# Linear attention gated by a squared-ReLU MLP: masks later on GpSimd, and three small matmul groups in another tile mode

## The chip, the cores and the metric

The kernel runs on one core of a Trainium2 chip. The metric is the time of one execution on the device, in microseconds (us): the median of several runs. Durations of single instructions come from one profiled execution, in which times count from the start of the span (first to last instruction of the core). The engines are named as the profile names them: PE is TensorE (PEld its weight loads), DVE is VectorE, ACT is ScalarE, POOL is GpSimd, and SP is the queue that issues nearly all DMAs.

## What is computed

For 2048 tokens of width 448, in bfloat16 (weights wqkv, wo, w1, w2; 16 heads of 28; hidden width 1792):

```python
xn = _layernorm(x, axis=-1)
q, k, v = heads(xn @ wqkv)
phi = lambda t: jnp.where(t > 0, t + 1, jnp.exp(t)) + 1e-6
kv = jnp.einsum("bhsd,bhse->bhde", phi(k), v)
z = jnp.einsum("bhsd->bhd", phi(k))
num = jnp.einsum("bhqd,bhde->bhqe", phi(q), kv)
den = jnp.einsum("bhqd,bhd->bhq", phi(q), z)[..., None] + 1e-6
s = merge_heads(num / den) @ wo
r = relu(xn @ w1 + b1)
g = silu((r * r) @ w2 + b2)
return x + s * g
```

(`heads` and `merge_heads` stand for the reshapes of the reference.)

## The kernel before

**Tiling.** The tokens are 16 tiles of 128 (index si), in 4 groups of 512 (g) or 2 halves of 1024 (u). The width 448 is three blocks of 128 and a rest of 64 (c = 0 to 3). The normalized tile xn has 512 columns: its last 64 are stored twice, so that after transposition the rest lies on rows 0 to 63 of block 3 of xT and again on rows 64 to 127. The weights' rest rows are loaded twice too (`load_k`, lines 420 to 426), once into each half. Two 64-row matmuls on two different results can so run side by side on the two halves of TensorE; `pe_four` (line 509) does that for four results at a time.

**Stages.** Line 1108 runs 43 matmuls on a zero tile (`wz`) ahead of the real work. Tiles 0 to 3 are normalized on VectorE (`ln_stats` 465, `ln_norm` 483, the copy of the 64 columns in `dup` 713) and transposed on TensorE (`x_transpose0` 726, matmuls of line 737, copies back in lines 757 and 763); later tiles are transposed by DMA (line 500). The first hidden units H0.0 to H0.6 are computed in pieces (`pe_part` 572, matmuls of line 701), as soon as parts of xT and of w1 are there. Then follow, in groups of four results, K (phi(k), token-major, line 622), Q (phi(q), transposed, line 646) and H (hidden units, line 705), with the first four gates G (line 977) among them. ScalarE takes the exponentials and the ReLU, VectorE the rest of phi (lines 605 and 612), the squares (686) and the gate's sum with b2 (994).

**q rests.** Column block 384 to 447 of q, the fourth of the transposed q, has only 64 output rows. `qx(u)` (line 653) computes it for even tiles into PSUM rows 0 to 63 and for odd tiles into rows 64 to 127, side by side. Its contraction runs over three 128-row blocks, and over rows 0 to 63 of the fourth.

**z.** GpSimd adds up phi(k) over the 16 tiles (`zsum`, line 628; sums of line 632, the last into `zb`). `z_cols` (line 840) turns zb into columns by matmuls against a column of ones: three with 128 columns of zb (line 846) and two with the 64 of the rest, for rows 0 to 63 and 64 to 127 (line 851). Three VectorE products (line 863) with `zmask` spread them over heads into `zsb`, the weights of `den` (line 895, matmuls of line 900).

**Masks.** `zmask`, `hmask` (used in `fold_wv`, line 832) and `ehd` (used in `spread`, line 938) are made of memsets on VectorE and 14 `affine_select` on GpSimd (line 359): eight for zmask, four for ehd, two for hmask. They are added to the program right after the identity and have no wait for any other work but their memsets.

**The last gate.** For tile 15 the bias b2 is added on TensorE: `gg` with `part` (line 967) begins with one matmul of a row of ones (`onesr`) and row 0 of `b2b` (line 975), then the 14 matmuls of the gate, in two pieces between the last output matmuls (line 1067). SiLU reads the result from PSUM (line 989).

**Order.** The program is a list of operations with reads and writes. The order on PE and SP is the order of the list. For ACT, DVE and POOL a list scheduler (`schedule`, line 88) with an estimated cost for each operation picks the order, the eight PSUM banks, and the engine where there is a choice. An engine carries out its list strictly in order, and an operation waits for the semaphores of what it needs.

Of the kernel before, what the change touches and what calls it, by code (L numbers as in the profile page):

```python
# [6 lines left out]
ALU = mybir.AluOpType  # L7
AF = mybir.ActivationFunctionType

P = 128  # L10
S, D, F = 2048, 448, 1792
NT, NG, NF = S // 128, S // 512, F // 128
NH, DH = 16, 28
# [281 lines left out]
def bass_recurrent_scan__linear_attn_block__dense_activation_squared_relu__prompt_kernel(  # L295
    nc, A_x, A_wqkv, A_wo, B_x, B_w1, B_b1, B_w2, B_b2, out
):
    with ExitStack() as es:
# [8 lines left out]
        zmask = sb("zmask", [P, 5, 32], f32)  # L307
        ones = sb("ones", [P, 1], bf)
        wz = sb("wz", [P, P], bf)
        onesr = sb("onesr", [1, P], bf)  # L310
        ehd = sb("ehd", [P, D], bf)
        x_tok = sb("x_tok", [P, NT, D], bf)
        xn = sb("xn", [P, NT, 512], bf)
        xT = sb("xT", [P, NT, 4, P], bf)
        w_qkv = sb("w_qkv", [P, 4, 3 * D], bf)
# [12 lines left out]
        pqx = sb("pqx", [P, 2, 4, P], bf)  # L328
        pk = sb("pk", [P, NT, D], bf)
        zacc = sb("zacc", [P, D], f32)  # L330
        zb = sb("zb", [P, D], bf)
        at = sb("at", [P, 4, D], bf)
        eps5 = sb("eps5", [P, 1], f32)
        r2 = sb("r2", [P, NF, S], bf)
# [11 lines left out]
        def pool(fn, writes, reads=(), dur=0.3):  # L346
            add("pool", fn, reads, writes, dur)
# [4 lines left out]
        def bcast(ap, reps):  # L352
            return free_ap(ap, [[0, reps]] + list(ap.ap[1:]))

        def select(view, name, pattern, base, cm, fill, op=ALU.is_ge, dur=0.3):
            masks.append(
                add(
                    "pool",
                    lambda e, _: e.affine_select(
                        out=view, in_=view, pattern=pattern, compare_op=op, fill=fill, base=base, channel_multiplier=cm  # L360
                    ),
                    [name], [name], dur,
                )
            )

        masks = []
        pool(lambda e, _: e.memset(ident[:, :], 0.0), ["ident"])
        select(ident[:, :], "ident", [[-1, P]], 0, 1, 1.0, ALU.not_equal)
        pool(lambda e, _: e.memset(eps5[:, :], 1e-5), ["eps5"], dur=0.1)
# [1 line left out]
        def vset(ap, val, name, again=False, dur=0.08):  # L371
            add("dve", lambda e, _: e.memset(ap, val), [name] if again else [], [name], dur)

        vset(wz[:, :], 0.0, "wz")
        vset(onesr[:, :], 1.0, "onesr")
        vset(zsb[:, :, :], 0.0, "zsb0")
        vset(hmask[:, :], 1.0, "hmask", dur=0.15)
        vset(zmask[:, :, :], 1.0, "zmask", dur=0.2)
        vset(ehd[:, :], 0.0, "ehd", dur=0.3)
        vset(kvm[:, :, :], 0.0, "kvm", dur=1.0)  # L380
        pool(lambda e, _: e.memset(eps6[:, :], 1e-6), ["eps6"], dur=0.1)

        def late_constants():
            hv = hmask[:, :].rearrange("p (b j) -> p b j", b=HC)
            select(hv, "hmask", [[-DH, HC], [0, DH]], 0, 1, 0.0)
            select(hv, "hmask", [[DH, HC], [0, DH]], DH - 1, -1, 0.0)
            for view, pat, base in (
                (zmask[:, 0:3, :], [[P, 3], [-DH, 32]], 0),
                (zmask[:, 3, :], [[-DH, 32]], 384),
                (zmask[:, 4, :], [[-DH, 32]], 320),  # L390
            ):
                select(view, "zmask", pat, base, 1, 0.0)
                select(view, "zmask", [[-a, n] for a, n in pat], DH - 1 - base, -1, 0.0)
            select(zmask[:, 3, :], "zmask", [[0, 32]], 63, -1, 0.0)
            select(zmask[:, 4, :], "zmask", [[0, 32]], -64, 1, 0.0)
            pool(lambda e, _: e.memset(ones[:, :], 1.0), ["ones"], dur=0.1)
            ev = ehd[:, :].rearrange("p (h j) -> p h j", h=NH)
            for g in range(NG):
                select(ev, "ehd", [[-1, NH], [0, DH]], -32 * g, 1, 1.0, ALU.not_equal, dur=0.6)

        tok = lambda t, lo, hi: t[0].rearrange("(p s) d -> p s d", s=NT)[:, lo:hi, :]

# [56 lines left out]
            load_k("sp", w_qkv, A_wqkv, "wv", 2 * D, 3 * D)  # L459

        add("act", lambda e, _: e.preload_act_table_set("natural_log_exp_and_others"), [], ["actw"], 1.3).prio = -2000.0
        masks.clear()
        late_constants()

        def ln_stats(si, hold=()):
            op = add("dve", lambda e, _: e.bn_stats(st6[:, si, :], x_tok[:, si, :]), [("x", si)], [("st", si)], 0.58)  # L466
# [161 lines left out]
        def zsum(i):  # L628
            o = zb if i == NT - 1 else zacc
            add(  # L630
                "pool",
                lambda e, _: e.tensor_tensor(  # L632
                    out=o[:, :], in0=pk[:, 0, :] if i == 1 else zacc[:, :], in1=pk[:, i, :], op=ALU.add
                ),
                [("pk", i), ("pk", 0) if i == 1 else "zacc"], ["zb" if i == NT - 1 else "zacc"], 1.05,
            )

        for si in range(4):
            pr.alias(("xT", si), [("xTp", si // 2 * 2, c) for c in range(4)])
# [13 lines left out]
        def qx(u):  # L653
            b = Buf("QX")

            def f(e, _):
                last = None
                for c in range(4):
                    rw = slice(0, 128) if c < 3 else slice(0, 64)
                    for o in (0, 1):  # L660
                        last = e.matmul(  # L661
                            ps(b)[64 * o : 64 * o + 64, 0:512], w_qkv[rw, c, 384:448],
                            xT[rw, 8 * u + o : 8 * u + 8 : 2, c, :], start=(c == 0), stop=(c == 3),
                        )
                return last

            add("pe", f, xnames(2 * u) + xnames(2 * u + 1) + wnames("wq"), [b], 4 * MM(512) + 0.1)
            phi(b, pqx[:, u, :, :].rearrange("p a b -> p (a b)"), ("pqx", u), 512)

        def h_out(b, g, fi):  # L670
# [169 lines left out]
        def z_cols():  # L840
            b = Buf("Z")

            def f(e, _):
                last = None
                for c in range(3):
                    last = e.matmul(
                        ps(b)[:, c : c + 1], zb[:, c * P : (c + 1) * P], ones[:, :], start=(c == 0), stop=True,
                        skip_group_check=True,
                    )
                for o in (0, 1):  # L850
                    last = e.matmul(
                        ps(b)[64 * o : 64 * o + 64, 3 + o : 4 + o], zb[:, 384:448], ones[:, :], start=False, stop=True,
                        skip_group_check=True,
                    )
                return last

            add("pe", f, ["zb", "ones"], [b], 0.35)
            for v, c0, c1, lo, hi in ((0, 0, 3, 0, 128), (1, 3, 4, 0, 64), (2, 4, 5, 64, 128)):

                def zops(e, _, c0=c0, c1=c1, lo=lo, hi=hi):  # L860
                    z = ps(b)[lo:hi, c0:c1]
                    z = free_ap(z, [[1, c1 - c0], [0, 32]])
                    return e.tensor_tensor(out=zsb[lo:hi, c0:c1, :], in0=z, in1=zmask[lo:hi, c0:c1, :], op=ALU.mult)

                add("dve", zops, [b, "zmask", "zsb0"], [("zsb", v)], 0.2)


        def fold_wo(c):
            b = Buf("M")
# [25 lines left out]
        def den():  # L895
            def f(e, _):
# [16 lines left out]

            add(
                "pe", f,
                [("zsb", v) for v in range(3)] + [("pq", g, c) for g in range(NG) for c in range(3)]
                + [("pqx", u) for u in (0, 1)],
                [denb], 4 * 0.24,
            )
# [47 lines left out]
        def gg(si, b=None, part=None):  # L967
            b = b or Buf("G")
            g = si // 4
            fis = range(NF) if part is None else part  # L970

            def f(e, _):
                last = None
                if part is not None and fis[0] == 0:
                    last = e.matmul(ps(b)[:, 0:D], onesr[:, :], b2b[0:1, :], start=True, stop=False)
                for fi in fis:
                    last = e.matmul(  # L977
                        ps(b)[:, 0:D], r2[:, fi, si * P : (si + 1) * P], w_2[:, fi, :],
                        start=(fi == 0 and part is None), stop=(fi == NF - 1),
                    )  # L980
                return last

            rd = [("r2", g, fi) for fi in fis] + ["w2"] + (["b2b", "onesr"] if part is not None else [])
            add("pe", f, rd + ([b] if fis[0] else []), [b], len(fis) * MM(D) + (0.19 if part is not None else 0))
            gs = gbuf[:, si % NGB, :]
            if part is not None:
                if fis[-1] == NF - 1:
                    add(
                        "act", lambda e, _: e.activation(out=gs, in_=ps(b)[:, 0:D], func=AF.Silu), [b, "acts"],
                        [("g", si % NGB)], 0.576,  # L990
                    )
            else:
                add(
                    "dve", lambda e, _: e.tensor_tensor(out=gs, in0=ps(b)[:, 0:D], in1=b2b[:, :], op=ALU.add),  # L994
                    [b, "b2b"], [("g", si % NGB)], 0.624,
                )
# [108 lines left out]
                x_transpose(si, si + step)  # L1105
            pr.lead = 0.0

        warm(43, 0.106)
        H0 = {fi: hh(0, fi, fi >= 7) for fi in range(NF)}
        pr.hot = -100.0  # L1110
        ln_stats(0)
# [18 lines left out]
            pe_part([H0[i] for i in range(4)], 0, (c,))  # L1130
        pe_part([H0[i] for i in range(4, 6)], 0)
        t23 = x_transpose0(2)
        for op in masks:
            op.hold = [t23]
        pr.hot = None
        pe_part([H0[6]], 0)
        for c in range(3):
# [10 lines left out]
        load_w1(3, "sp", "sp")  # L1148
        load_x(8, 12)
        ln(4, 8, lead=3, hold=[t23])  # L1150
        load_x(12, 16)
        dma("sp", w_2[:, :, :], B_w2.rearrange("(f p) d -> p f d", p=P), ["w2"], F * D * 2)
        late_loads()
# [13 lines left out]
            zsum(i)  # L1167
        gg(2)
        gg(3)
        quads("H2.8 H2.9 H2.10 H2.11 Q1.1 H2.12 Q1.2 H2.13")  # L1170
        quads("K3.0 H3.0 K3.1 H3.2 K3.2 H3.1 K3.3 H3.3")
        for i in range(12, 16):
# [77 lines left out]
```

## Time and profile before

| | |
|---|---|
| median of 6 runs | 148.42 us (148.17 to 149.26) |
| the profiled execution | 148.17 us |
| its span, first to last instruction | 146.4 us |
| PE busy | 141.1 us (96% of the span) |
| DVE, ACT, POOL busy | 96.2, 79.4, 34.5 us |
| granted TensorE clock | 1.0 in the whole span |
| masks on POOL (line 359, from 1.56) | zmask 2.30, ehd 3.13, hmask 0.66 us |

The profile lists for each engine its instructions with start and duration. "Idle before <- X" names what ended the wait in front of an instruction; "issue" is a wait for nothing that the profile shows. The tile mode of a matmul or weight load stands as rows*columns ahead of its shape: 128*128 is the whole array, 128*64 a half of its columns, 64*64 a quarter. Matmuls are pipelined: starts are more telling than durations. The chain of work that ended last follows the waits back from the end.

### The profile page before, as it was taken

To read this page: it belongs to the slowest core of one execution; us is meant where nothing else is said; L and a number is where in the kernel's file an instruction comes from. 1 tells how busy PE (TensorE), PEld (TensorE's weight loads), DVE (VectorE), ACT (ScalarE), POOL (GpSimd) and SP (SyncE) were. 2 spreads that over 40 slices of the span, in tenths; PEclk is the share of its full clock that TensorE was granted. 3 is DMA by queue.
4 is the path that set the end of the run, shared out by engine and by line. 5 is a ranking of instruction groups with operands and counts; after the bars stand their busy time and mean duration, and the time that the engine had idled before them with its cause. 6 is when DMAs were issued, how large, how long until landed. Compare 5 with 4: busy or idle time off the path is not lost.

```text
span 146.4 us, 2838 instructions
## 1 busy us (share of the span) xinstructions
PE 141.1 (96%) x1127; PEld 70.2 (48%) x1127; DVE 96.2 (66%) x222; ACT 79.4 (54%) x152; POOL 34.5 (24%) x50
## 2 busy tenths in 40 slices
PE   7799999999999999999999999999999999999990
PEld 7675444444444444444443554364444545545450
DVE  6979878899978995268999310089675426136343
ACT  3618888987986980487879613997211110210200
POOL 6800026570000650001550000000001909109100
PEclk9999999999999999999999999999999999999999
DMA  3977699934802500000000000000000211102212
GB/s 85 323 229 222 150 240 377 322 107 87 61 0 43 100 4 0 0 0 4 2 0 0 4 0 0 0 7 0 0 0 0 66 64 63 63 0 63 67 63 63
DMA packets 16025, 10.53 MB, mean 72 GB/s; under 512 B 7372, under 2 KB 15628, under 8 KB 16012
## 3 DMA queue, kind: packets, MB, share of 16 engines
q1 hardware_dynamic: 15824, 10.28, 26.9%
q8 instruction: 9, 0.15, 0.5%
q10 hardware_dynamic: 188, 0.07, 0.2%
q14 instruction: 4, 0.03, 0.1%
HBM read 6.94 MB, written 1.84 MB: 60 GB/s over the span
## 4 chain that ended last, share of the span: by engine, by line
PE 93%; DVE 3%; DMA 1%; ACT 0%; issue 0%; DVEq 0%
PE pb L977 30%; PE pb L705 26%; PE pb L622 7%; PE pb L793 6%; PE pb L646 6%; PE pb L1031 6%; PE pb L701 3%; PE pb L1067 2%; PE pb L661 2%; DMA x_tok<-in_A_x_dram 1%; PE pb L799 1%; PE pb L878 1%; DVE st L466 1%; PE pb L737 1%; PE pb L938 1%; PE pb L822 1%
## 5 line engine op out<-in xcount | busy, mean ns | idle before, releaser
L977 PE MATMUL pb<-w,r 128*128 128x448 bf16 x224 | 44.3, 353 | 0.0
L672 ACT ACTIVATE r<-pb,b1f 128x512 bf16<-128x512 f32 x54 | 33.8, 690 | 10.6 <-PE pb L705 10.6
L705 PE MATMUL pb<-xT,w 64*128 64x512 bf16 (+1 forms) x291 | 38.5, 376 | 0.0
L977 PEld LDWEIGHTS pb<-w,r 128*128 128x128 bf16 x224 | 21.1, 98 | 21.1 <-issue 2.0
L1004 ACT ACTIVATE gbuf<-gbuf 128x448 bf16<-128x448 bf16 x15 | 8.5, 580 | 29.7 <-DVE gbuf L994 29.7
L632 POOL TENSOR_TENSOR zacc<-zacc,pk 128x448 f32<-128x448 f32 x13 | 14.6, 1124 | 39.8 <-DVE pk L612 36.5
L1020 POOL TENSOR_TENSOR obuf<-obuf,x_tok 128x448 bf16<-128x448 bf16 x12 | 12.0, 1031 | 48.7 <-DVE obuf L1014 48.7
L705 PEld LDWEIGHTS pb<-xT,w 64*128 64x128 bf16 (+1 forms) x291 | 14.2, 94 | 16.6 <-issue 0.4
L994 DVE TENSOR_TENSOR gbuf<-pb,b2b 128x448 bf16<-128x448 f32 x15 | 9.4, 624 | 16.6 <-PE pb L977 16.5
L686 DVE TENSOR_TENSOR r<-r 128x512 bf16<-128x512 bf16 x35 | 16.6, 513 | 3.0 <-ACT r L672 3.0
L1014 DVE TENSOR_TENSOR obuf<-pb,gbuf 128x448 bf16<-128x448 f32 (+2 forms) x17 | 9.2, 591 | 7.2 <-PE pb L1031 4.7
L622 PE MATMUL pb<-w_qkv,xT 64*128 64x448 bf16 x112 | 13.2, 349 | 0.0
L961 DVE TENSOR_TENSOR pqT<-pqT,pb 128x512 bf16<-128x512 bf16 x12 | 7.4, 682 | 8.6 <-PE pb L938 8.6
L687 ACT ACTIVATE r<-r 128x512 bf16<-128x512 bf16 x21 | 12.6, 634 | 0.0
L646 PE MATMUL pb<-xT,w_qkv 64*128 64x512 bf16 x84 | 11.0, 376 | 0.0
L705 PE MATMUL pb<-xT,w_1r 64*128 64x512 bf16 x56 | 10.3, 377 | 0.0
L612 DVE SCALAR_TENSOR_TENSOR pk<-pb,pk 128x448 bf16<-128x448 f32 x16 | 9.9, 624 | 0.5
L466 DVE BATCH_NORM_STATS2 st<-x_tok 128x6 f32<-128x448 bf16 x16 | 9.2, 615 | 1.2 <-DMA x_tok<-in_A_x_dram 1.2
L600 ACT ACTIVATE pk<-pb 128x448 bf16<-128x448 f32 x16 | 7.8, 541 | 3.9 <-PE pb L622 3.9
L793 PE MATMUL pb<-pk,xn 128*128 128x448 bf16 x48 | 9.4, 353 | 0.0
L612 DVE SCALAR_TENSOR_TENSOR pqT<-pb,pqT 128x512 bf16<-128x512 f32 x12 | 8.2, 689 | 0.3
L622 PEld LDWEIGHTS pb<-w_qkv,xT 64*128 64x128 bf16 x112 | 5.4, 94 | 6.1 <-issue 0.4
(90 smaller groups left out, 126.0 us busy)
## 6 DMA issues: line engine op xcount, KB each, us to landing
out_dram<-obuf SPq DMA_DIRECT2D x15, 112.0 KB, 1.8
w<-in_B_w_dram SPq DMA_DIRECT2D x1, 1568.0 KB, 10.1
x_tok<-in_A_x_dram SPq DMA_DIRECT2D x3, 448.0 KB, 4.1
w<-in_B_w_dram SPq DMA_DIRECT2D x3, 384.0 KB, 4.2
w_qkv<-in_A_wqkv_dram SPq DMA_DIRECT2D x3, 336.0 KB, 5.7
w_o<-in_A_wo_dram SPq DMA_DIRECT2D x1, 392.0 KB, 9.4
w_qkv<-in_A_wqkv_dram SPq DMA_DIRECT2D x6, 56.0 KB, 5.1
x_tok<-in_A_x_dram SPq DMA_DIRECT2D x2, 112.0 KB, 2.1
```

The costliest lines, as they stand in the source:

```text
L466: op = add("dve", lambda e, _: e.bn_stats(st6[:, si, :], x_tok[:, si, :]), [("x", si)], [("st", si)], 0.58)
L612: lambda e, _: e.scalar_tensor_tensor(out=slot, in0=ps(buf)[:, 0:n], scalar=1.0 + 1e-6, in1=slot, op0=ALU.add, op1=ALU.max),
L622: return e.matmul(ps(b)[:, 0:D], xT[rw, si, c, :], w_qkv[rw, c, D : 2 * D], start=start, stop=stop)
L632: lambda e, _: e.tensor_tensor(out=o[:, :], in0=pk[:, 0, :] if i == 1 else zacc[:, :], in1=pk[:, i, :], op=ALU.add),
L646: return e.matmul(ps(b)[:, 0:512], w_qkv[rw, c, m * P : (m + 1) * P], xT[rw, 4 * g : 4 * g + 4, c, :], start=start, stop=stop,)
L672: rl = lambda e, _: e.activation(out=slot, in_=ps(b)[:, 0:512], func=AF.Relu, bias=b1f[:, fi : fi + 1])
L686: return e.tensor_tensor(out=slot, in0=slot, in1=slot, op=ALU.mult)
L687: return e.activation(out=slot, in_=slot, func=AF.Square)
L705: return e.matmul(ps(b)[:, 0:512], lhs, xT[rw, 4 * g : 4 * g + 4, c, :], start=start, stop=stop, skip_group_check=not full,)
L793: last = e.matmul(ps(b)[:, 0:D], xn[:, si, c * P : (c + 1) * P], pk[:, si, :], start=(si == 0), stop=(si == NT - 1),)
L977: last = e.matmul(ps(b)[:, 0:D], r2[:, fi, si * P : (si + 1) * P], w_2[:, fi, :], start=(fi == 0 and part is None), stop=(fi == NF - 1),)
L1020: lambda e, _: e.tensor_tensor(out=ob, in0=ob, in1=x_tok[:, si, lo:hi], op=ALU.add),
```

## The change

- **Masks.** The zmask selects now wait for the last copy of the transposed tiles 2 and 3 (line 763), the ehd and hmask selects for the sum of the fourth gate (line 994, si = 3); in the built order they lie on POOL ahead of the first zacc sum, and between the sums of tile 11 and tile 12.
- **q rests.** A new tile `wqh` holds the fourth block of the q weights times 0.5, made by VectorE on both halves of the rows. The fourth pass of `qx` uses all 128 rows: both copies of the rest times half the weight each.
- **z columns.** `zb` grows to 512 columns, of which the last 64 repeat the rest (a copy on POOL). All five matmuls take 128 columns; the last two take the same ones. One VectorE product with zmask makes the whole of zsb.
- **Last gate.** The bias matmul takes the identity and all of b2b instead of one row.
- The memsets of onesr and zsb are gone, the memset of wz is put first by priority, that of ones is added earlier. The warm-up has 40 matmuls instead of 43.

On PE, SP and ACT the built order is the same but for these edits, and the PSUM banks are the same. On DVE, wqh stands after the second ReLU of line 677 and ahead of the squares.

```diff
+        wqh = sb("wqh", [P, 64], bf)
-        zb = sb("zb", [P, D], bf)
+        zb = sb("zb", [P, 512], bf)
...
         vset(wz[:, :], 0.0, "wz")
-        vset(onesr[:, :], 1.0, "onesr")
-        vset(zsb[:, :, :], 0.0, "zsb0")
+        pr.ops[-1].prio = -1e6
...
-        def late_constants():
+        def z_masks(after):
...
-                select(view, "zmask", pat, base, 1, 0.0)
-                select(view, "zmask", [[-a, n] for a, n in pat], DH - 1 - base, -1, 0.0)
+                select(view, "zmask", pat, base, 1, 0.0, after=after)
+                select(view, "zmask", [[-a, n] for a, n in pat], DH - 1 - base, -1, 0.0, after=after)
...
+        def head_masks(after):
...
-                select(ev, "ehd", [[-1, NH], [0, DH]], -32 * g, 1, 1.0, ALU.not_equal, dur=0.6)
+                select(ev, "ehd", [[-1, NH], [0, DH]], -32 * g, 1, 1.0, ALU.not_equal, dur=0.6, after=after)
...
+            if i == NT - 1:
+                pool(lambda e, _: e.tensor_copy(zb[:, D:512], zb[:, 384:D]), ["zbd"], ["zb"], dur=0.25)
...
-                    rw = slice(0, 128) if c < 3 else slice(0, 64)
                     for o in (0, 1):
                         last = e.matmul(
-                            ps(b)[64 * o : 64 * o + 64, 0:512], w_qkv[rw, c, 384:448],
-                            xT[rw, 8 * u + o : 8 * u + 8 : 2, c, :], start=(c == 0), stop=(c == 3),
+                            ps(b)[64 * o : 64 * o + 64, 0:512], w_qkv[:, c, 384:448] if c < 3 else wqh[:, :],
+                            xT[:, 8 * u + o : 8 * u + 8 : 2, c, :], start=(c == 0), stop=(c == 3),
                         )
...
+            if u == 0:
+                add(
+                    "dve",
+                    lambda e, _: e.tensor_scalar(
+                        out=wqh[:, :], in0=w_qkv[:, 3, 384:448], scalar1=0.5, scalar2=None, op0=ALU.mult
+                    ),
+                    wnames("wq"), ["wqh"], 0.1,
+                )
...
-                for c in range(3):
+                for c in range(5):
+                    k = min(c, 3) * P
                     last = e.matmul(
-                        ps(b)[:, c : c + 1], zb[:, c * P : (c + 1) * P], ones[:, :], start=(c == 0), stop=True,
-                        skip_group_check=True,
-                    )
-                for o in (0, 1):
-                    last = e.matmul(
-                        ps(b)[64 * o : 64 * o + 64, 3 + o : 4 + o], zb[:, 384:448], ones[:, :], start=False, stop=True,
+                        ps(b)[:, c : c + 1], zb[:, k : k + P], ones[:, :], start=(c == 0), stop=True,
                         skip_group_check=True,
                     )
...
+            z = lambda: free_ap(ps(b)[:, 0:5], [[1, 5], [0, 32]])
+            add(
+                "dve", lambda e, _: e.tensor_tensor(out=zsb[:, :, :], in0=z(), in1=zmask[:, :, :], op=ALU.mult),
+                [b, "zmask"], ["zsb"], 0.25,
+            )
...
-                    last = e.matmul(ps(b)[:, 0:D], onesr[:, :], b2b[0:1, :], start=True, stop=False)
+                    last = e.matmul(ps(b)[:, 0:D], ident[:, :], b2b[:, :], start=True, stop=False)
...
-        warm(43, 0.106)
+        warm(40, 0.107)
...
-        for op in masks:
-            op.hold = [t23]
...
+        z_masks([("xTp", 2, 3)])
...
+        head_masks([("g", 3)])
```

## The prediction

> **What bounds the kernel now.** I read the page's busy times first, then the chain that ended last, then TensorE's waits.
>
> ```profile
> PE 141.1 (96%) x1127; PEld 70.2 (48%) x1127; DVE 96.2 (66%) x222; ACT 79.4 (54%) x152; POOL 34.5 (24%) x50
> PE 93%; DVE 3%; DMA 1%; ACT 0%; issue 0%; DVEq 0%
> ```
>
> ```profile
> PE pb L1081 <- DVE wz L372: 1.1, 1, 1.1
> PE pb L737 <- DVE xn L486: 0.7, 1, 0.7
> ```
>
> TensorE works in 141.1 of 146.4 us and is 93% of the chain. Its only listed waits lie ahead of the first transposes (5.68). From there to 143 us it is fed without a listed gap, so the change can gain in two ways only: start that stream earlier, or take TensorE time out of it. It can lose by making TensorE wait.
>
> **Tile modes inside the stream.** A weight load shows rows*columns. The loads around the first q rest (line 661), then the matmuls around the z columns (846, 851) and around the last gate's bias (975):
>
> ```profile
> 37.34 0.36 PEld L661 LDWEIGHTS pb<-xT,w_qkv 128*64 128x64 bf16 x6 [0.42 <-issue]
> 38.11 0.11 PEld L661 LDWEIGHTS pb<-xT,w_qkv 64*64 64x64 bf16 x2 [0.41 <-issue]
> 38.45 0.11 PEld L977 LDWEIGHTS pb<-w,r 128*128 128x128 bf16 x2 [0.23 <-issue]
> ```
>
> ```profile
> 86.11 0.22 PE L846 MATMUL pb<-ones,zb 128*128 128x1 bf16 x3
> 86.25 0.19 PE L851 MATMUL pb<-ones,zb 128*64 128x1 bf16 x2
> 86.38 0.36 PE L793 MATMUL pb<-pk,xn 128*128 128x448 bf16 x1
> ```
>
> ```profile
> 138.09 0.73 PE L1067 MATMUL pb<-msb,pqT 128*128 128x448 bf16 x3
> 138.75 0.36 PE L975 MATMUL pb<-b2b,onesr 1*128 1x448 bf16 x1
> 139.04 0.36 PE L977 MATMUL pb<-w,r 128*128 128x448 bf16 x1
> ```
>
> Each change of the second number or the first is a point where the next weights are not loaded under the matmul before ("issue" idle).
>
> *q rests, twice.* A pair of 512-column matmuls streams in 0.217 (eight of line 646 take 1.03, the last alone 0.38: 0.65 over three pairs). The 64*64 pair of the rests takes 38.45 - 38.11 = 0.34, so 0.12 goes to one mode change. The change runs this pair as 128*64: three changes become two. At 78.94 the rows repeat (79.70 to 80.04: 0.34). Gain 2 x 0.12 = 0.24. A 128-row pair isn't dearer: the three ahead take 38.11 - 37.34 = 0.77 = 3 x 0.217 + 0.12.
>
> A rule speaks against this edit: the Trainium skill, "TensorEngine Tiling (Array Packing)", Theoretical Speedup, promises up to twice the speed for a contraction of 64 rows or fewer in its own tiles; its Key Properties say that a change of mode drains the engine. By the first, a 64-row pair costs half a 128-row one, 0.11, and filling it up gives 0.11 away each time: 0.24 - 0.22 leaves 0.02. The row decides: only two of the four 64*64 tiles were used, and the pair took longer than a 128-row one, not half.
>
> *z columns.* Three full-mode one-column matmuls start (0.22 - 0.163)/2 = 0.03 apart. All five take 86.38 - 86.11 = 0.27 with two mode changes; five in full mode 5 x 0.03 = 0.15. Gain 0.12 (nothing if a full weight load showed at the 0.056 spacing of the warm-up matmuls).
>
> *Last bias.* A 448-column matmul streams in 0.19 (four of line 977: 0.92, the last alone 0.35). From the third of line 1067 (138.09 + 2 x 0.19 = 138.47) to the gate's first at 139.04 are 0.57 for two of them: 0.57 - 0.38 = 0.19 gained with identity and b2b on 128 rows.
>
> These 0.55 us lie in TensorE's own stream. Everything behind, the last SiLU and line 1014 included, follows TensorE, so they should reach the end.
>
> **The start.** VectorE makes the first tiles while GpSimd writes masks:
>
> ```profile
> 4.81 0.53 DVE L722 COPY xn<-xn 128x64 bf16<-128x64 bf16 x1
> 5.24 0.38 DVE L486 TENSOR_SCALAR xn<-x_tok,mv,rstd 128x448 bf16<-128x448 bf16 x1
> ...
> 7.76 0.18 DVE L722 COPY xn<-xn 128x64 bf16<-128x64 bf16 x1
> ```
>
> The same copy of 64 columns takes 0.53 beside GpSimd's ehd selects (3.82 to 6.95) and 0.18 without them. The Trainium skill, "SBUF — State Buffer", Who interferes with whom, has it that VectorE's two-port modes and GpSimd exclude each other for a whole instruction. By that rule both line 486 too might wait, up to 0.67 each (one select); by the rows they (0.36 at 4.41, 0.38 at 5.24) are as short as later ones (0.40). I take the row: 0.35, not 1.7. The transposes at 5.68 move to 5.33.
>
> What is late next? Two transfers, whose issue and landing do not move. The first block of w1 is issued at 2.2 and lands 4.2 later, 6.4: line 701 begins at 6.45 instead of 6.66. The second:
>
> ```profile
> L404 SPq DMA_DIRECT2D w<-in_B_w_dram x1: 668/668/668, 2.8 to 2.8; - x1
> ...
> DMA to landing us min/median/max: 5.0/5.0/5.0
> ```
>
> It lands at 7.8 to 7.9. The thirteenth matmul of line 701, the first to need it, already starts at 6.66 + 12 x 0.11 = 7.98, just behind it. So 0.30 of the 0.35 turns into a wait for this block. What stays is the 0.05 that the second transposes wait for VectorE's copy (8.69, six matmuls of 0.11 after 7.98 end at 8.64). Gain 0.05; ends: 0, and 0.35 if the block lands early.
>
> **The rest, at nothing.** 43 warm-up matmuls become 40: 0.17 of filler ahead of a wait for VectorE; the remaining pause is 0.67 - 0.35 + 0.17 = 0.49, shorter than today's, after which the matmuls run at full clock. Two memsets less on VectorE end before x lands (2.70 and 2.92). The zmask selects (2.3 us) now follow the last transposed copy (10.17), beside four bn_stats, which took 0.59 to 0.63 beside selects at 2.92 to 6.46 and about as much without; zmask is needed at 86.5. The ehd and hmask selects (3.13 + 0.66) follow the fourth gate's sum (line 994, ends 58.78); queued behind them on GpSimd is the zacc sum of 68.94: 6 us to spare, without that up to 3.8. VectorE's squares at 61.37 to 63.5 may each lose up to a select (0.67); their readers come after 112, and 0.77 idle follows. The new zb copy (at most 0.3, by a small select) ends near 75.5; z columns read it at 86.1. One zsb product instead of three, with 2.4 us before line 900. SP and ACT keep their orders.
>
> **The new wait.** The halved weights (wqh) are one small VectorE copy that waits for wq's three DMAs. In the built order it stands behind the second ReLU of line 677 (ends 15.47). The last wq DMA is issued at 12.4 and lands 4.9 later, 17.35. VectorE, in order, stands still until then; behind it are two squares and the exponent work of K tiles 1 and 0, which release the banks of Q0.0/Q0.1 and of H0.12/H0.13.
>
> ```profile
> 16.80 0.28 DVE L605 TENSOR_SCALAR pk<-pk 128x448 bf16<-128x448 bf16 x1 [0.66 <-ACT pk L600]
> ...
> 17.95 0.62 DVE L612 SCALAR_TENSOR_TENSOR pk<-pb,pk 128x448 bf16<-128x448 f32 x1
> 19.55 0.63 DVE L466 BATCH_NORM_STATS2 st<-x_tok 128x6 f32<-128x448 bf16 x1 [0.97 <-DMA x_tok<-in_A_x_dram]
> ```
>
> After: copy 17.38, squares 17.5 and 17.8, then the four operations of lines 605 and 612 from 18.15, the two of 612 ending at 19.1 and 19.95 instead of 17.73 and 18.57. TensorE takes the banks at 19.50 and 20.36 (a little earlier after). 0.35 is left: it costs nothing, just. The lag of 0.3 at 19.55 goes into idle time near 24.9.
>
> **Sum.** 0.24 + 0.12 + 0.19 + 0.05 = 0.60. The profiled execution took 148.17 (146.4 of span, 1.8 around it), the lowest of the runs; it becomes 147.57. From the median, 148.42 - 0.60 = 147.8.
>
> **Rivals and chances.** *As summed*: 147.8 (147.55 to 148.0), 0.45. *The start pays in full*: w1's second block lands by 7.6, so all 0.35 arrive: 0.55 + 0.35, 147.5; 0.20. Against it is the landing above. *Locks fall badly*: VectorE's two short operations at 23.1 and 23.3, now 0.3 later, meet a zacc sum (about 1.1 us each), as line 486 at 30.84 does (four in 2.83); their bank has 1.1 us. Half the gain gone: 148.1; 0.17. *The mode changes only move elsewhere*, the weight loads being late anyway: 0.05 left, 148.35; 0.06. *Slower: wq lands late.* The price is one for one from 17.7 on; beyond 18.3 the whole gain is eaten. Landings of w_qkv go up to 9.2 us after issue; one of 6.6 (landing 19.0) costs 1.3: 149.1; 0.12. For it: many transfers share 11 to 18 us. Against it: the two before landed within 5.7.
>
> The 8-in-10 range is 147.35 to 148.6. Half a per cent (0.74 us), about what can be told from no change here, separates the classes: faster (below 147.68) is most of the second case and two fifths of the first, 0.36; slower (above 149.16) is half of the last and what I can't see, 0.12; same, 0.52.
>
> **What would show it.** Line 661's successor: four loads of pairs 0.22 apart, next load 0.98 after the first, not 1.11. Z columns within 0.15. The bias and the gate 0.19 apart. L722 at 0.18, and a gap on TensorE before the thirteenth matmul of line 701. VectorE idle from 15.5 to 17.4 on a w_qkv DMA. I am wrong if TensorE then waits near 19.5 or 20.4, or if a mode change is as dear without a 64*64 pair.

## The result, and the profile after

The kernel after takes 147.76 us (median of 28 runs, 147.37 to 148.52), the kernel before 148.63 (65 runs in the same comparison, 148.14 to 150.03). The ratio is 0.9946, 95% interval 0.9934 to 0.9958: by it 0.80 us less, 0.54%. Runs over 1.5% above the fastest of their kernel are left out of the ratios. The profiled execution of after took 147.72 us with a span of 146.0.

The predicted time, 147.8, is 0.04 off, and that nearness is partly luck: the prediction took 0.60 from the median of six runs, 148.42; the many runs put before 0.21 higher, and the gain at 0.80.

The page of after (busy times, then the chain of waits), and TensorE's waits:

```profile
PE 141.5 (97%) x1124; PEld 71.3 (49%) x1124; DVE 96.0 (66%) x219; ACT 79.2 (54%) x152; POOL 35.3 (24%) x51
...
PE 96%; DVE 1%; ACT 0%; issue 0%; DVEq 0%
```

```profile
PE pb L1077 <- DVE wz L368: 1.1, 1, 1.1
```

TensorE's wait for VectorE ahead of the first transposes is no longer listed. Its busy time is larger (141.5 against 141.1) while the span is shorter: its first matmuls were slower in this execution, as shown below.

The loads around the first q rest, then the matmuls around the z columns and around the last bias (lines 657, 851 and 971 now):

```profile
37.55 0.36 PEld L657 LDWEIGHTS pb<-xT,w_qkv 128*64 128x64 bf16 x6 [0.42 <-issue]
38.01 0.11 PEld L657 LDWEIGHTS pb<-xT,wqh 128*64 128x64 bf16 x2
38.53 0.49 PEld L973 LDWEIGHTS pb<-w,r 128*128 128x128 bf16 x4 [0.41 <-DVE pqT L600]
```

```profile
86.07 0.27 PE L851 MATMUL pb<-ones,zb 128*128 128x1 bf16 x5
86.20 1.10 PE L797 MATMUL pb<-pk,xn 128*128 128x448 bf16 x5
```

```profile
138.47 0.35 PE L971 MATMUL pb<-b2b,ident 128*128 128x448 bf16 x1
138.66 0.73 PE L973 MATMUL pb<-w,r 128*128 128x448 bf16 x3
```

From the first load of the rests to the next line's are 0.98 (38.53 - 37.55; before 1.11); from the z columns to the next line are 0.13 (0.27); the bias starts 0.19 ahead of the gate (0.29).

VectorE at the start, and at the halved weights:

```profile
4.43 0.36 DVE L481 TENSOR_SCALAR xn<-x_tok,mv,rstd 128x448 bf16<-128x448 bf16 x1
4.83 0.18 DVE L726 COPY xn<-xn 128x64 bf16<-128x64 bf16 x1
5.11 0.40 DVE L481 TENSOR_SCALAR xn<-x_tok,mv,rstd 128x448 bf16<-128x448 bf16 x1
...
15.97 0.18 DVE L666 TENSOR_SCALAR wqh<-w_qkv 128x64 bf16<-128x64 bf16 x1 [0.30 <-DMA w_qkv<-in_A_wqkv_dram]
```

The copy of 64 columns takes 0.18 (0.53), the next line 481 begins 0.28 after it (0.43), and VectorE waits 0.30 for wq.

**Where the time went.** The first matmul of K (line 622, now 617) parts the execution: ahead of it lies the start, behind it TensorE's stream. Worked out from matmul starts in the traces, with the lowest time of each kernel's runs beside them (the execution least held up), in us:

| kernel | first K matmul | from it to the last matmul | lowest time | median |
|---|---|---|---|---|
| before, first profile | 13.83 | 128.94 | 148.14 | 148.63 |
| before, second profile | 14.63 | 128.94 | 148.16 | 148.53 |
| after, first profile | 14.03 | 128.34 | 147.37 | 147.76 |
| after, second profile | 14.13 | 128.34 | 147.39 | 147.77 |
| after, 43 warm-ups | 13.81 | 128.34 | 147.39 | 147.80 |
| tile modes only | 14.29 | 128.43 | 147.54 | 148.02 |
| start only (late masks, 40 warm-ups) | 14.28 | 128.94 | 148.03 | 148.46 |
| late masks only | 14.27 | 129.27 | 148.01 | 148.43 |
| late masks only, again | 14.12 | 129.09 | 147.99 | 148.45 |
| 40 warm-ups only | 16.16 | 128.94 | 148.15 | 148.50 |

The stream (from the first K matmul to the last matmul) shows the tile modes: 128.94 without them, 128.34 with them, to 0.01, but for 0.09 to 0.33 that three executions add. All three lose it at one place, the ninth matmul of the stream, and there the second half of w1's second rest block had just landed: at 15.26 (late masks only), 14.92 (the same again) and 15.03 (tile modes only), each time 0.09 ahead of that matmul; in before's first profile it landed at 14.11, 0.47 ahead. So a late transfer adds this, not the modes. The start varies by 0.8 between two executions of the same code (before), and is later still in one (16.16). So one profile can measure the modes and can't measure the start.

### The profile page after: what moved, and what is told of

Same layout as the page of the kernel before. It is cut to its first block, busy times and chain, and to the rows that moved or that the text cites. A ratio compares the mean times of both kernels' runs of the same rounds, so it can differ in the third digit from the quotient of the medians.

```text
span 146.0 us, 2829 instructions
## 1 busy us (share of the span) xinstructions
PE 141.5 (97%) x1124; PEld 71.3 (49%) x1124; DVE 96.0 (66%) x219; ACT 79.2 (54%) x152; POOL 35.3 (24%) x51
## 4 chain that ended last, share of the span: by engine, by line
PE 96%; DVE 1%; ACT 0%; issue 0%; DVEq 0%
PE pb L973 30%; PE pb L709 26%; PE pb L617 7%; PE pb L797 6%; PE pb L643 6%; PE pb L1027 6%; PE pb L1077 3%; PE pb L705 3%; PE pb L657 1%; PE pb L1063 1%; PE pb L803 1%; PE pb L874 1%; PE pb L741 1%; PE pb L934 1%; PE pb L826 1%; PE pb L896 1%
## 5 line engine op out<-in xcount | busy, mean ns | idle before, releaser
L709 PE MATMUL pb<-xT,w_1r 64*128 64x512 bf16 x56 | 10.3, 377 | 0.0
```

The costliest lines, as they stand in the source:

```text
L709: return e.matmul(ps(b)[:, 0:512], lhs, xT[rw, 4 * g : 4 * g + 4, c, :], start=start, stop=stop, skip_group_check=not full,)
```

## Experiments

My theory: the three mode edits give their 0.60 on TensorE; the late masks give the rest, in the executions where TensorE waits for VectorE's chain. The rivals: the warm-ups pay, not the masks; or the modes only move elsewhere and the start pays all. The median of before differs by 0.4 us between the comparisons below (148.76, 148.8 and 148.4), so each ratio is taken within one comparison.

**The kernel after, again.** No edit.

> The changed kernel once more, on the same chip as the three partial ones. In its first profile the mode edits paid 0.58 us, but line 705 began 0.20 us LATER than line 701 before, because the 40 warm-up matmuls ran at the slow spacing of 0.107 throughout, where before 26 did and the rest at 0.056. Theory 1 (the moment of full clock is drawn anew at each execution; it differs by up to some 3 us, and the start is worth about 0.2 us on average): 0.80 us faster than before again, and this profile may show another number of slow warm-up matmuls. Theory 2 (the change itself makes the clock late): again 40 slow ones, line 705 again near 6.86, and the gain is 0.4.

Ratio 0.9942 (0.9922 to 0.9962), 147.77 us. Here wq landed later:

```profile
17.05 0.18 DVE L666 TENSOR_SCALAR wqh<-w_qkv 128x64 bf16<-128x64 bf16 x1 [1.22 <-DMA w_qkv<-in_A_wqkv_dram]
```

VectorE stood 1.22 instead of 0.30, and the stream is the same 128.34: no matmul of the stream waited for it.

**Tile modes only.** The kernel after with masks early and 43 warm-ups:

```diff
+        early_at = len(pr.ops)
+        z_masks([])
+        head_masks([])
+        early_masks = pr.ops[early_at:]
...
-        warm(40, 0.107)
+        warm(43, 0.106)
...
+        for op in early_masks:
+            op.hold = [t23]
```

> The three tile-mode edits alone: masks at the start as before, 43 warm-up matmuls. Theory 1: the mode edits' own 0.58 us (q rests 0.24, z columns 0.14, bias 0.20) and nothing at the start: ratio to before 0.9961. Theory 2: the same 0.58 or a little more. Rival 3 (the mode edits are worth the whole measured 0.80, the start nothing): 0.9946.

Ratio 0.9963 (0.9944 to 0.9982), -0.55 us by the ratio; the lowest run is 0.60 under that of before. The modes give what they take out of the stream. (The other small edits of after, the memsets, stay in.)

**The start only.** Late masks and 40 warm-ups, with q rests, z columns and bias as before (the three edits of the diff undone).

> The other part alone: masks moved, 40 warm-up matmuls, but q rests, z columns and bias as before. Theory 1: the measured 0.80 less the 0.58 of the modes, 0.2 us faster: 0.9985; line 722's copy 0.18 instead of 0.53. Prediction as written: 0.05 faster, since w1's second block lands at 7.9: 0.9997. Theory 2: slower by 0.2.

Ratio 0.9987 (0.9969 to 1.0005): about -0.2 us, not told from nothing.

**After, with 43 warm-ups.**

```diff
-        warm(40, 0.107)
+        warm(43, 0.106)
```

> The changed kernel with 43 warm-up matmuls instead of 40. Prediction as written: filler ahead of a wait, no change against the changed kernel. Theory 1: none in executions that get the full clock early, but where all warm-up matmuls are slow, three of them are 0.32 us that the first transposes wait for; on average 0.1 to 0.15 us slower than the changed kernel, still 0.65 faster than before.

Ratio 0.9939 (0.9921 to 0.9956), as with 40. This kernel and the tile modes alone were in the same comparison and differ only in when the masks are made: medians 147.80 and 148.02, so about 0.2 us for the late masks. TensorE at the start of this execution:

```profile
1.06 3.92 PE L1077 MATMUL pb<-wz 128*128 128x128 bf16 x43 [1.06 <-DVE wz L368]
...
6.72 1.47 PE L705 MATMUL pb<-xT,w 128*128 128x256 bf16 x12 [0.27 <-DMA w<-in_B_w_dram]
```

With the copy short, a DMA is next late, as predicted, but it is w1's first block, which landed at 6.58.

**Late masks only, twice.** The kernel before with the masks of after (and, not in the lines below, the first place of wz's memset and the earlier memset of ones):

```diff
-        late_constants()
...
+        z_masks([("xTp", 2, 3)])
...
+        head_masks([("g", 3)])
```

> The kernel before with nothing but the later masks (43 warm-up matmuls, q rests, z columns and bias as before). Theory 1 (the copy's 0.35 us is covered, by w1's landing where the clock is full early, by the warm-up matmuls where it is full late): at most 0.1 us faster, ratio 0.9993 or above, although line 722's copy takes 0.18. Rival 4 (the lock on the copy was the start's whole cost, as the gap between the two partial kernels with and without early masks, 0.36 us, hints): 0.35 us faster, 0.9976.

> The same code as the run with the late masks alone, again, to see whether its -0.35 us holds. Theory A (the late masks pay): ratio again 0.9975 to 0.998, about 148.4 against 148.75. Theory B (that was a draw of the start's other conditions: clock, landing of x tile 1 and of w1): ratio within 0.0015 of the run of the kernel before against itself. In the profile the copy of 64 columns of tile 1's transposition lasts 0.18 instead of 0.53 either way; with a late clock and 43 warm-ups K(0,0) should still start at 14.2 to 14.3.

Ratios 0.9977 (0.996 to 0.9994), then 0.9994 (0.9977 to 1.001). The first draw's 0.35 us did not hold. The mean of the three ratios with late masks and the old modes (0.9987, 0.9977, 0.9994) is 0.9986: 0.2 us. Two of the three intervals reach past 1, so one run alone doesn't settle it. Their lowest runs are 0.11 to 0.14 under the lowest of before in the same comparison.

**40 warm-ups only, and before against itself.**

```diff
-        warm(43, 0.106)
+        warm(40, 0.107)
```

> The kernel before with one number changed: 40 warm-up matmuls instead of 43; masks and tile modes as before. Theory A (the late masks pay the start's gain; the warm-ups are filler ahead of w1's first block): no change, ratio 1.000, within 0.0015 of the run of the kernel before against itself. Theory B (the three warm-ups pay: where the full clock comes late, 3 x 0.107 = 0.32 us less stand ahead of the first transposition): about half to all executions gain 0.15 to 0.3, so 148.4 to 148.5 against 148.75, ratio 0.998 to 0.999. In the profile: if its full clock is later than about 6 us, K(0,0) starts near 14.0 to 14.1 (43 warm-ups with a late clock gave 14.27); with an early clock near 13.8.

> The kernel before against itself: ratio 1.000, and its interval shows what these comparisons can tell, some 0.0015. A second profile of it: the masks lock the 64-column copy at 0.5 again if the mechanism is steady. If the reading is right that the first profile had an early full clock (3.75 us) and the latest landing of w1's second block (7.88), this one, with a later clock or an earlier landing, should show the copy's 0.35 on TensorE: the first matmul of H(0,0) follows the copy and not the DMA, and the execution's span is then longer, 146.7 to 147.3.

Ratios 1.0004 (0.9992 to 1.0017) and 1.0005 (0.9989 to 1.002): three warm-ups less give nothing that can be told. The second profile of before tells more than its time. VectorE's rows in it, and GpSimd's selects beside them:

```profile
4.76 0.67 DVE L486 TENSOR_SCALAR xn<-x_tok,mv,rstd 128x448 bf16<-128x448 bf16 x1
5.46 0.68 DVE L722 COPY xn<-xn 128x64 bf16<-128x64 bf16 x1
6.04 0.39 DVE L486 TENSOR_SCALAR xn<-x_tok,mv,rstd 128x448 bf16<-128x448 bf16 x1
...
3.82 3.13 POOL L359 TENSOR_SCALAR_AFFINE_SELECT ehd<-ehd 128x448 bf16<-128x448 bf16 x4
```

Line 486 begins 0.35 later than in the first profile (x tile 1 landed at 3.98, not 3.43), and now both it (0.67 instead of 0.36) and the copy (0.68) stand beside selects. Overlapping instructions must be read by their starts. From the start of the first line 486 to that of the second, the copy between them, it is 0.68 in all ten profiles with late masks (4.43 to 5.11 in after). With early masks it is 0.83 (before's first profile: 4.41 to 5.24), 0.83 (tile modes only), 0.97 (40 warm-ups only) and 1.28 here: the masks cost VectorE's chain 0.15, 0.15, 0.29 and 0.60, by where the selects fall. The first K matmul is 0.80 later than in the first profile (14.63 against 13.83): 0.35 of it is x, 0.45 the selects. TensorE's rows of this execution, then of the profiled one with 40 warm-ups:

```profile
1.05 4.63 PE L1081 MATMUL pb<-wz 128*128 128x128 bf16 x43 [1.05 <-DVE wz L372]
...
6.48 0.62 PE L737 MATMUL pb<-ident,xn 128*128 128x128 bf16 x8 [0.69 <-DVE xn L486]
...
7.46 2.14 PE L701 MATMUL pb<-xT,w 128*128 128x256 bf16 x18
```

```profile
1.05 4.45 PE L1081 MATMUL pb<-wz 128*128 128x128 bf16 x40 [1.05 <-DVE wz L372]
...
6.48 1.04 PE L737 MATMUL pb<-ident,xn 128*128 128x128 bf16 x8 [0.86 <-DVE xn L486]
...
7.78 3.42 PE L701 MATMUL pb<-xT,w 128*128 128x256 bf16 x18
```

Both begin the transposes at 6.48. In the first, 43 warm-ups took 4.63: the last of them at the fast spacing. In the other all 40 were slow (0.107 apart), TensorE paused, and the same 18 matmuls took 3.42 instead of 2.14; first K matmul 16.16 instead of 14.63, time 150.47, by far the slowest of its 11 runs. The full clock came only behind 10.3, and this cost 1.5 us. After's first profile, whose 40 warm-ups were as slow but which had no pause, was at full clock from 7.0. So the pause may be what put it off, but two executions don't show it.

**The q rest as the second of the four passes.** The kernel after with the 64-row rest unscaled, four mode changes for each group instead of two:

```diff
-                for c in range(4):
+                for c in (0, 3, 1, 2):
+                    rw = slice(0, 128) if c < 3 else slice(0, 64)
```

> The changed kernel with the q rests on 64 rows as before, but as the second of the four passes instead of the last, so that each of the two groups has four mode changes instead of two. If a mode change costs 0.12 us wherever it stands: 4 x 0.12 = 0.48 us slower than the changed kernel, ratio to before 0.9942 + 0.0032 = 0.9974, and the loads of the next line 0.96 + 0.24 after the first of the group. If the price was that of a 64*64 pair and not of the change: 0.24 slower, as when it stands last.

```profile
37.49 0.11 PEld L658 LDWEIGHTS pb<-xT,w_qkv 128*64 128x64 bf16 x2 [0.42 <-issue]
37.83 0.11 PEld L658 LDWEIGHTS pb<-xT,w_qkv 64*64 64x64 bf16 x2 [0.23 <-issue]
38.16 0.14 PEld L658 LDWEIGHTS pb<-xT,w_qkv 128*64 128x64 bf16 x4 [0.23 <-issue]
38.72 0.49 PEld L966 LDWEIGHTS pb<-w,r 128*128 128x128 bf16 x4 [0.41 <-issue]
```

From the first load to the next line's are 1.23 instead of 0.98: two changes more, 0.25, or 0.12 each (if a pair streams in 0.217, its step into the 64*64 mode, 0.34, and the one out of it, 0.33, hold one change each). The stream is 0.48 longer (128.81), the median 0.54 longer than after's (148.30), the ratio to before 0.9956 (0.9934 to 0.9977, expected 0.9974). So here a mode change costs the same both ways. That the 64-row pair streams no faster is read from line 646's pairs in the prediction, which have 64 rows too (64*128) and take 0.217; these loads alone can't part the pair from its changes.

**w1's first block by ScalarE's queue.** The kernel after, to have the block earlier:

```diff
-        load_w1(0, "sp", "act")
+        dma(
+            "act", w_1[:, :, 0:512], B_w1[0:384, 0:512].rearrange("(c p) j -> p c j", p=P), [("w1", 0, 0)], 768 * 512,
+        )
+        load_w1r(0, "act")
```

> The changed kernel with w1's first block issued by ScalarE's queue ahead of the first rests, so that it and the second block, next on SP, are issued 0.7 us earlier. Where the full clock comes early, the third partial kernel waited 0.27 us for the first block (landing 6.58) and started the thirteenth matmul at 8.02. If these landings cap the start: that wait gone and 0.2 to 0.3 us gained in executions with an early clock, 0 in late ones; on average 0.1 to 0.15, ratio to before 0.993. If they don't: no difference to the changed kernel, 0.9942.

Ratio 0.9969 (0.995 to 0.9988), 148.36 us: slower than after by 0.6 in the median, by 0.4 in the lowest run. My expectation missed. TensorE's rows:

```profile
6.72 2.19 PE L708 MATMUL pb<-xT,w 128*128 128x256 bf16 x18 [0.23 <-ACT xT L764]
9.17 0.62 PE L744 MATMUL pb<-ident,xn 128*128 128x128 bf16 x8 [0.26 <-DVE xn L729]
```

Line 708 no longer waits for the DMA, but for ScalarE's copy, and the second transposes wait 0.26 for VectorE. That takes back what the block gives. The other 0.3 lies behind the first K matmul (stream 128.65), and 0.22 of it at 23.2:

```profile
21.11 1.15 DVE L464 BATCH_NORM_STATS2 st<-x_tok 128x6 f32<-128x448 bf16 x2 [0.45 <-DMA x_tok<-in_A_x_dram]
23.21 0.49 PEld L620 LDWEIGHTS pb<-w_qkv,xT 64*128 64x128 bf16 x8 [0.54 <-DVE pk L610]
```

An x block was issued at 17.03 and landed at 21.09 (15.09 and 19.89 in after). VectorE, in order, waited 0.45 for it, so its line 610 ended later, and the loads of the next K group waited for that line. wq was late too (VectorE stood 2.18 us for it, until 18.12), but VectorE had caught up at 20.66, before the x block came. Why these transfers were late is not shown.

**wqh made later.** It waits for K tile 3 as well, so that VectorE doesn't stand at 15.7:

```diff
-                    wnames("wq"), ["wqh"], 0.1,
+                    wnames("wq") + [("pk", 3)], ["wqh"], 0.1,
```

> The changed kernel with the halved weights made later in VectorE's order (after the phi of K tile 3, some 23 us), where wq has long landed. The wait of VectorE for wq's DMA near 16 us (0.3 to 1.2 us in four profiles) should be gone. Prediction as written: that wait costs TensorE nothing, so no difference to the changed kernel, 0.9942. Rival: in executions where wq lands late it reaches TensorE, 0.1 to 0.2 us faster than the changed kernel.

147.74 us in 7 runs (ratio 0.9917, 0.9884 to 0.995), the stream 128.34: the new wait costs the stream nothing in after.

**Three mode changes and a matmul more taken out.** The kernel after, with the fourth token sum right behind the second q rests (both are 128 x 64) and the last fold of w_o in the full mode, its 64 columns of kv doubled:

```diff
-        kvm = sb("kvm", [P, 4, D], bf)
+        kvm = sb("kvm", [P, 4, 512], bf)
...
+                "dve", lambda e, _: e.tensor_copy(kvm[0:PD, 3, D:512], kvm[0:PD, 3, 384:D]), ["kvd"], ["kvx"], 0.12,
...
-                for o in range(1 if c < 3 else 2):
-                    dst = ps(b)[:, 0:D] if c < 3 else ps(b)[64 * o : 64 * o + 64, 0:D]
-                    wd = P if c < 3 else 64
...
+        token_sum(3)
...
-        token_sum(3)
```

> The kernel after with two more mode changes taken out: the fourth token sum is put right behind the second group of q rests, so that both use the 128 x 64 mode in a row (one change of mode less, 0.12 us), and the last fold of w_o is made in the full mode, its 64 columns of kv doubled to 128 (two changes less, 2 x 0.12, one matmul less of about 0.19 for the heads it held apart, against one VectorE copy that lies beside other work). Theory A (every change of mode on TensorE's path costs 0.12 wherever it stands): 0.12 + about 0.2 = 0.3 us less than after, some 147.45 against 147.76, ratio to before about 0.992. Theory B (there TensorE waits for VectorE or GpSimd, and the changes lie inside waits): as after, ratio 0.994.

147.29 us (147.15 to 147.47, 5 runs), ratio 0.9929 (0.9909 to 0.9948): the fastest kernel here, though its interval overlaps that of after. Its rows at the rests, and at the fold:

```profile
79.36 0.38 PE L657 MATMUL pb<-xT,wqh 128*64 128x512 bf16 x2
79.58 1.68 PE L803 MATMUL pb<-pk,xn 128*64 128x448 bf16 x16
...
98.96 1.50 PE L874 MATMUL pb<-w_o,kvm 112*128 112x448 bf16 x7
100.29 2.81 PE L973 MATMUL pb<-w,r 128*128 128x448 bf16 x14
```

The token sum follows the rests by 0.22, the plain streaming time, with no change between; the fold takes 1.33 (98.96 to 100.29) against 1.55 in after. The stream is 128.07, 0.27 less than after: 0.12 and 0.22 gained, 0.08 given back at 94.6, where the step from the small matmuls of line 934 to those of line 826 takes 0.41 instead of 0.33: TensorE now comes to line 826 before ScalarE has ended a ReLU (line 676, at 94.96) that its load waits for. By the ratios the gain over after is 0.25 us, which the stream alone makes up; the median's other 0.2 goes with before's, which was lower by as much in this comparison (148.40 against 148.63).

## Why the prediction came out as it did

**Tile modes: right, with each size.** Summed 0.24 + 0.12 + 0.19 = 0.55, measured 0.60 in the stream: twice 0.12 at the rests, 0.16 at the z columns, 0.20 at the bias. Each rest group lost one mode change, the z columns and the bias two each, so one change was worth 0.12, 0.08 and 0.10. Where the Trainium skill ("TensorEngine Tiling (Array Packing)", Theoretical Speedup) spoke for the 64-row tiles, the row was right: with only two of four tiles in use the pair is no faster, and the drain that its Key Properties name has a price here, 0.08 to 0.12.

**The start: two terms failed, against each other.** The first is "I take the row: 0.35, not 1.7". It subtracted the copy's durations, 0.53 - 0.18; but the next instruction began only 0.43 after the copy began, against 0.28 without selects. By the starts, that execution lost 0.15, and the transposes, forecast for 5.33, began at 5.56 in after. The second is "So 0.30 of the 0.35 turns into a wait for this block. What stays is the 0.05". The cap is there, but it takes little: in the earliest start of all (the last experiment) the thirteenth and fourteenth matmul of line 705 come 0.13 and 0.12 after the ones before them, where 0.11 is the rule, so 0.03 goes to w1's second block, and the first K matmul still stands 0.13 earlier than in before (13.70 against 13.83). In after itself there is no gap at the thirteenth matmul at all. So in an execution like the one profiled the term is 0.13, not 0.05; the lowest runs with late masks say 0.11 to 0.14.

In the median it is more, about 0.2. I put that down to the profiled execution being one of the quickest of before: in the second profile, with x tile 1 later, the selects cost 0.60, and everything that the cap was made of had long landed. Two profiles don't show how common that is. In that second profile the rule of the Trainium skill that I set aside for the row ("SBUF — State Buffer", Who interferes with whom) is partly borne out: line 486 itself took 0.67, as long as a select. Still, no profile comes near the 1.7 of the rule. That the modes give 0.60 is shown by the stream. That the rest, about 0.2, is the masks' is shown less firmly: it is what is left, the three ratios say it together, and so does the pair 147.80 and 148.02, but each of these ratios is known only to some 0.25 us either way.

**Warm-ups as filler: right in the time** (1.0004, 0.9992 to 1.0017), wrong in the picture: "the remaining pause is 0.49", "after which the matmuls run at full clock". In after's first profile there was no pause at all, since its 40 warm-ups took longer (4.45) than the 43 of before (3.85). Before, then after:

```profile
1.05 3.85 PE L1081 MATMUL pb<-wz 128*128 128x128 bf16 x43 [1.05 <-DVE wz L372]
...
5.68 0.62 PE L737 MATMUL pb<-ident,xn 128*128 128x128 bf16 x8 [0.67 <-DVE xn L486]
```

```profile
1.05 4.45 PE L1077 MATMUL pb<-wz 128*128 128x128 bf16 x40 [1.05 <-DVE wz L368]
...
5.56 1.04 PE L741 MATMUL pb<-ident,xn 128*128 128x128 bf16 x8
```

**Masks late, zb copy, zsb product: nothing behind the start**, as predicted: the stream of the start-only kernel is 128.94 as in before, and what after's loses is accounted for by the three mode edits to 0.01. **The wait for wq:** predicted until 17.35, seen in after until 15.97 and 17.05, and until 18.12 with w1's block on ScalarE's queue; the claim that TensorE's reserve covers it held each time, and the slower rival never came from this wait. **Rivals:** "only move elsewhere" is refuted by the stream; "locks fall badly" shows nowhere; the start in full (0.35) is above what the mean shows, though one execution of before lost 0.60 there.

## What to carry to other kernels

Cut a trace where the start ends, and compare the stream behind it: it repeats to 0.01 us unless a transfer comes late in it, while the start differs by 0.8 between executions of one kernel. Price a delayed instruction by when the next one starts, not by its own duration (0.35 against 0.15 here). A cap that rests on one landing of one DMA is a draw; take an early and a late start as two cases. And count changes of tile mode along TensorE's list: each cost 0.08 to 0.12 here, and duplicating 64 rows or columns to fill the mode was cheaper than changing it.

## What I had not expected of the hardware

TensorE's full clock begins at another moment in each execution: by the spacing of the warm-ups (0.107, then 0.056) between 3.7 and 7.0 us of the span in thirteen profiles, that is 2.7 to 6.0 after the first matmul, and once behind 10.3. The profile's row of the granted clock shows 1.0 all the while; only the warm-ups' row shows it (40 in 4.45, 43 in 3.85). The Trainium skill, "TensorE: Matmul & The Clock Gate", What's actually happening, explains it by a free-running window of 3.413 us in which TensorE must be busy. The two executions with slow warm-ups throughout fit it: the spacing drops at about 7.0 us in after and at about 10.4 with 40 warm-ups only, where a pause fell in between, one window later. The scatter of 500 ns that the page gives is smaller than the one here.
